# Numerators of a linear attention as whole float32 products, with new input layouts and a new order of issue

## The chip, the cores and the metric

The kernel runs on one NeuronCore of a Trainium2 chip. The metric is the device time of one execution in microseconds. The engines are TensorE (PE; its weight loads are shown as PEld), VectorE (DVE), ScalarE (ACT), GpSimd (POOL) and SyncE (SP), which issues all DMAs here.

## The reference

An attention with random features over 4 batches, 8 heads, 576 rows and 64 columns, and behind it two dense layers over 2304 tokens (512 to 2048 to 512), the first with the gate `h * sigmoid(h)`, the second with `h * cos(h)`.

```python
def phi(x):
    proj = np.einsum('bhsd,df->bhsf', x, w_phi)            # 64 -> 128
    proj = proj - np.max(np.abs(proj), axis=-1, keepdims=True)
    return np.concatenate([np.exp(proj), np.exp(-proj)], axis=-1)
q_p, k_p = (phi(q), phi(k))
kv = np.einsum('bhsf,bhsd->bhfd', k_p, v)
z = np.sum(k_p, axis=2)
num = np.einsum('bhsf,bhfd->bhsd', q_p, kv)
den = np.einsum('bhsf,bhf->bhs', q_p, z)[..., None] + 1e-06
x = (num / den)            # to 2304 x 512, then
h = x @ w_in;  y = (h / (1 + np.exp(-h))) @ w_out          # and the second layer with h * cos(h)
```

## The kernel before

The heads are worked on in eight groups of four (`NQ`, half a batch each). Within a group, heads 0 and 2 are pair p = 0 and heads 1 and 3 are pair p = 1. The 576 rows of a head are 512 in four tiles of 128, and a tail of 64; the tails of four heads are unit u = 0, and a head's four tiles are one of the units 1 to 4.

The steps of a group, each a "piece of work" with a name in the order lists:

- `T` (lines 270 to 286): TensorE transposes the loaded q or k; ScalarE copies PSUM to the high part `hi` (float32r, a float32 rounded to fewer bits that TensorE multiplies in one product); VectorE subtracts for the low part `lo`.
- `phi` (290 to 307): three float32r products (hi x hi, hi x lo, lo x hi) of 256 columns for each row tile; VectorE takes the maximum of the absolute values and subtracts it, into SBUF.
- `kx` (311 to 317): ScalarE makes the keys' two exponentials, a unit at a time. `qx` (319 to 339): TensorE transposes the queries' differences, ScalarE makes the exponentials `e`, GpSimd rounds them to `qh`. `ql` (341 to 346): VectorE, or GpSimd for the tails, subtracts for the low part.
- `kv` (350 to 374): for a pair and a sign, one product for the tails and eight of 65 columns, in float32, with v beside a column of ones; at the end ScalarE copies the sums to `kv_hi` and VectorE makes `kv_lo`.
- `num` (376 to 395): four parts for a pair, each of six float32r products of 288 columns (high x high, high x low, low x high, for two signs); ScalarE copies a part to `xn`, and behind a pair's last part SP sends the row of denominators to a tile `den`.
- `inv` (179 to 189): VectorE inverts the denominators; they go to DRAM (`rd`) and come back on 64 partitions (`rb`). `app` (191 to 200): GpSimd multiplies, into the layers' input `xy`.
- `x`: a part of the first layer's inputs is split in two. `piece`: a quarter of the conversion of a weight tile (lines 91 to 128).

The order is written out by hand: `START` once, then `PERIOD` for n = -1 to 7. A + behind a name is the next group, ++ the one after that. Each engine takes its instructions in that order, and SP its DMAs. PSUM has 8 banks: 2 buffers `tp` of the input transposes, 2 of `phi`, 1 of `t2` (the queries' transposes), 3 that `kv` and `num` share. Where a tile has one buffer, as `qh`, `va` and the loaded inputs, the next group's write waits for the last reader.

The two layers (`moe`, lines 477 to 642) follow, all in float32r with three products each.

Of the kernel before, what the change touches and what calls it, by code (L numbers as in the profile page):

```python
# [30 lines left out]

MAGIC = 12582912.0
# [16 lines left out]
START = parse("""  # L49
T.k.2 w load.v T.k.0 T.k.1 load.k+ phi.k.0 kx.0 phi.k.1 T.q.0 phi.k.2 phi.k.3 kx.1 T.q.2 kv.0.0.0 kx.2 phi.k.4 kx.3  # L50
kv.0.0.1 phi.q.0 T.k.2+ kx.4 kv.1.0.0 phi.q.1 qx.0 T.q.1 phi.q.2 T.k.0+ kv.1.0.1 qx.1 phi.q.3 ql.1.g T.k.1+ kv.0.1.0
qx.2 phi.q.4 load.k++ ql.2.v kv.1.1.0 qx.3 ql.0.g kv.0.1.1 load.q+ kv.1.1.1 qx.4
# [3 lines left out]
kx.1+ x.2+ num.1.1 x.3+ phi.k.2+ T.k.0++ phi.q.0+ num.1.0 x.4+ load.q++ kx.2+ num.1.2 x.5+ kv.0.0.0+ inv.0 phi.k.0++  # L56
T.k.1++ T.q.2++ num.1.3 x.6+ qx.0+ piece phi.q.1+ ql.0.g+ phi.q.2+ kv.1.0.0+ kv.0.0.1+ piece qx.1+ phi.q.4+ app.0
kv.0.1.0+ qx.2+ ql.1.v+ inv.1 phi.q.3+ kv.0.1.1+ piece qx.4+ kv.1.0.1+ ql.2.v+ kv.1.1.0+ qx.3+ phi.k.3++ T.q.1++
kv.1.1.1+ load.k+++ num.0.0+ kx.0++ ql.3.v+ phi.k.4++ num.0.1+ T.k.2+++ load.v++ num.0.2+ x.0++ kx.3++ kx.4++
phi.k.1++ ql.4.v+ app.1 num.0.3+ x.1++ T.q.0++ piece  # L60
# [3 lines left out]
class Weights:  # L64
    """float64 weights, given as raw words, to float32 parts hi + lo of 12 and 12 bits."""
# [68 lines left out]
class Queue:  # L134
    """Pieces of the weights' conversion, taken one after the other."""
# [23 lines left out]
class Norm:  # L159
    """Numerators over denominators, to x, [dm, token]."""  # L160
# [30 lines left out]
    def apply(self, n, p):  # L191
        nc, xy = self.nc, self.xy
# [7 lines left out]
        nc.gpsimd.tensor_mul(xy[rows, B * NJ + b // 2, c0:c0 + 2, at], t[rows, :, SM:S], r[rows, :, SM:S])  # L200


def attention(tc, q, k, v, w_phi, norm, pieces, then):
    nc = tc.nc
    W = D + 1
    with ExitStack() as ctx:
# [5 lines left out]
        kr, krt, qr, qrt = {}, {}, {}, {}  # L212

        def load_qk(n, src, main, tails, name):
            b, h0 = divmod(n, 2)
            h0 *= 4
            t = fp.tile([P, 4, NJ, D], F32, name=f"{name}r")
            u = fp.tile([P, 2, D], F32, name=f"{name}rt")
            for i in range(2):
                nc.sync.dma_start(u[64 * i:64 * i + 64], src[b, h0 + 2 * i:h0 + 2 * i + 2, SM:S, :].rearrange("h s d -> s h d"))  # L220
            nc.sync.dma_start(t, src[b, h0:h0 + 4, 0:SM, :].rearrange("h (p j) d -> p h j d", j=NJ))
            main[n], tails[n] = t, u
# [33 lines left out]
        # Stationary operands of the last product: columns 0..64 [kv | z] of even heads, 63..127 [z | kv] of odd ones.  # L256
        kvs = [[sp.tile([P, 2, 2, M], F32R, name=f"kv{i}_{part}") for part in ("hi", "lo")] for i, M in enumerate((W, P))]
# [10 lines left out]
        tT = {}  # L268

        def transpose_in(n, name, i):  # L270
            main, tails = (kr, krt) if name == "k" else (qr, qrt)
            N = SM if i < 2 else P
            ps = pp.tile([P, N], F32, name="tp", tag="tp", bufs=2)
            if i < 2:
                for c in range(4):
                    x, jj = divmod(c, 2)
                    src = main[n][:, i + 2 * x, 2 * jj:2 * jj + 2, :].rearrange("p j d -> p (j d)")
                    nc.tensor.transpose(ps[:, c * P:(c + 1) * P], src, ident)
            else:
                nc.tensor.transpose(ps, tails[n].rearrange("p a d -> p (a d)"), ident)  # L280
            sfx = "m" if i < 2 else "t"
            hi = fp.tile([P, N], F32R, name=f"{name}T_hi{sfx}", bufs=2 if i < 2 else 1)
            lo = fp.tile([P, N], F32R, name=f"{name}T_lo{sfx}", bufs=2 if i < 2 else 1)
            nc.scalar.copy(hi, ps)
            nc.vector.tensor_sub(lo, ps, hi.bitcast(F32))
            tT[n, name, i] = (hi, lo)
# [3 lines left out]
        def phi(n, name, u):  # L290
            """Unit 0: the tails of the four heads; 1 + 2 p + x: head p + 2 x."""
            i = 2 if u == 0 else (u - 1) // 2
            ns = 1 if u == 0 else 2
            hi, lo = tT[n, name, i]
            ps = pp.tile([P, ns, 2 * F], F32, name="p", tag="p", bufs=2)
            for s in range(ns):
                c = 0 if u == 0 else (((u - 1) % 2) * 2 + s) * P
# [13 lines left out]
        def k_exp(n, u):  # L311
            src = pm.pop((n, "k", u))
            ns = 2 if u == 0 else 4
            t = sp.tile([P, 2, ns, F], F32, name="kpt" if u == 0 else "kp", bufs=1 if u == 0 else 4)
            nc.scalar.activation(t[:, 0], src, AF.Exp)
            nc.scalar.activation(t[:, 1], src, AF.Exp, scale=-1.0)
            kp[n, u] = t

        def q_exp(n, u):
            src = pm.pop((n, "q", u))  # L320
            ns = 2 if u == 0 else 4
            ps = pp.tile([P, ns, P], F32, name="t2", tag="t2", bufs=1)
            for i in range(ns):
                nc.tensor.transpose(ps[:, i, :], src[:, i, :], ident)
            if u == 0:
                for p in range(2):
                    qh[n, p] = sp.tile([P, 2, 2, S], F32R, name=f"qh{p}")
                    ql[n, p] = sp.tile([P, 2, 2, S], F32R, name=f"ql{p}")
            p, x = divmod(u - 1, 2)
            for c in range(2):  # L330
                e = sp.tile([P, ns, P], F32, name="et" if u == 0 else "e", bufs=2 if u == 0 else 4)
                nc.scalar.activation(e, ps, AF.Exp, scale=1.0 - 2.0 * c)
                if u == 0:
                    parts = [(e[:, i, :].rearrange("p (x s) -> p x s", x=2), *(t[n, i][:, c, :, SM:S] for t in (qh, ql))) for i in range(2)]
                else:
                    parts = [(e.rearrange("p a s -> p (a s)"), *(t[n, p][:, c, x, 0:SM] for t in (qh, ql)))]
                for i, (ev, hi, lo) in enumerate(parts):
                    nc.gpsimd.tensor_scalar(hi, ev, 1.0, 0.0, op0=ALU.mult, op1=ALU.add)
                    rests[n, u, c, i] = (lo, ev, hi)

        def q_rest(n, u, engine):
            """The lower parts of the queries' exponentials."""
            for c in range(2):
                for i in range(2 if u == 0 else 1):
                    lo, ev, hi = rests.pop((n, u, c, i))
                    engine.tensor_sub(lo, ev, hi.bitcast(F32))  # L346
# [356 lines left out]
```

## Time and profile before

| | us |
|---|---|
| median of 3 runs | 1051.86 |
| lowest and highest | 1050.23, 1052.01 |
| span of the profiled execution | 1048.8 |
| busy: TensorE, VectorE, ScalarE, GpSimd | 1019.1, 711.9, 407.8, 369.4 |

The profile is of one execution, and its own time is known only as the span, from the first recorded instruction to the last; the runs' median lies 3.1 us above it. TensorE's matmuls are pipelined: an instruction's duration holds the way through the array, so the distance between the starts of two neighbours is what one costs, and the busy time of a stretch is the time in which at least one is under way. A float32 product appears as more than one record. The granted clock is that of TensorE, 1.00 for 2.4 GHz.

### The profile page before, as it was taken

Reading aid. Unit: us, or ns where it says so; the run is one execution under the profiler, and the core shown is the slowest. Engines: PE = TensorE matmul, PEld = TensorE weight load, DVE = VectorE, ACT = ScalarE, POOL = GpSimd, SP = SyncE. Lnnn points to the kernel's source line nnn. Section 1 sums busy time; section 2 is a strip of 40 time slices with the busy share of each in tenths; the row PEclk is TensorE's granted clock in tenths of the full one; section 3 lists DMA queues with packets and bytes.
Section 4 is the critical chain, followed back from the end, with each engine's and each line's share of the span. In section 5 each row is a group of like instructions: output and inputs, shape, how many; then the busy total and the mean of one; then the engine's idle time right before and its main releaser. Section 6 shows DMA issues by size and latency. Waiting matters only on the chain.

```text
span 1048.8 us, 15083 instructions
## 1 busy us (share of the span) xinstructions
PE 1019.1 (97%) x6000; PEld 972.5 (93%) x6000; DVE 711.9 (68%) x956; ACT 407.8 (39%) x664; POOL 369.4 (35%) x426
## 2 busy tenths in 40 slices
PE   7999999999999999999999999999999999999998
PEld 7989999989999999999999999899888988998997
DVE  6999999978544344544545567667677867786764
ACT  5655566544433222222223333444333333333332
POOL 3566666656122111201211024334434433343221
PEclk9999999999999999999999999999999999999999
DMA  4544333114111101110110111101110111100112
GB/s 118 139 112 112 99 105 81 47 40 129 41 41 46 55 22 61 41 41 21 61 48 34 41 41 42 40 21 61 41 41 21 61 40 41 27 34 1 61 57 63
DMA packets 62757, 58.33 MB, mean 56 GB/s; under 512 B 30560, under 2 KB 55264, under 8 KB 62688
## 3 DMA queue, kind: packets, MB, share of 16 engines
q1 hardware_dynamic: 62688, 57.38, 18.5%
q8 instruction: 47, 0.77, 0.3%
q14 instruction: 22, 0.18, 0.1%
HBM read 52.49 MB, written 4.79 MB: 55 GB/s over the span
## 4 chain that ended last, share of the span: by engine, by line
PE 61%; DVE 25%; POOL 7%; ACT 4%; issue 1%; DMA 1%; SPq 0%; POOLq 0%; ACTq 0%; DVEq 0%
PE h L509 24%; PE y L558 6%; PE y L560 6%; PE y L559 6%; DVE ql L346 4%; DVE tb L531 3%; DVE tb L530 3%; DVE tb L535 3%; PE kv L363 3%; POOL ta L529 2%; PE y L563 2%; PE y L564 2%; PE y L565 2%; DVE xy L589 2%; POOL gh L536 2%; DVE gl L538 2%
## 5 line engine op out<-in xcount | busy, mean ns | idle before, releaser
L509 PE MATMUL h<-xh,win_hi 128*128 128x384 f32 x768 | 259.1, 337 | 1.7 <-DVE tb L535 1.7
L509 PE MATMUL h<-xl,win_hi 128*128 128x384 f32 x768 | 258.8, 337 | 0.3 <-DVE xl L474 0.3
L509 PE MATMUL h<-xh,win_lo 128*128 128x384 f32 x768 | 258.7, 337 | 0.0
L521 DVE SCALAR_TENSOR_TENSOR ta<-ta,h 128x768 f32<-128x768 f32 x48 | 45.8, 953 | 177.7 <-ACT ta L520 177.7
L509 PEld LDWEIGHTS h<-xh,win_hi 128*128 128x128 f32 x768 | 144.2, 188 | 4.7 <-PE y L565 2.6
L509 PEld LDWEIGHTS h<-xl,win_hi 128*128 128x128 f32 x768 | 144.2, 188 | 2.4 <-DVE xl L474 0.6
L509 PEld LDWEIGHTS h<-xh,win_lo 128*128 128x128 f32 x768 | 144.2, 188 | 0.0
L532 ACT ACTIVATE tb<-tb 128x768 f32<-128x768 f32 x48 | 40.7, 847 | 239.0 <-DVE tb L531 239.0
L558 PE MATMUL y<-gh,wout_hi 128*128 128x384 f32 x384 | 129.5, 337 | 0.2 <-ACT xy L587 0.2
L560 PE MATMUL y<-gh,wout_lo 128*128 128x384 f32 x384 | 129.6, 337 | 0.0
L559 PE MATMUL y<-gl,wout_hi 128*128 128x384 f32 x384 | 129.4, 337 | 0.0
L520 ACT ACTIVATE ta<-h 128x768 f32<-128x768 f32 x48 | 39.0, 813 | 206.4 <-PE h L509 203.1
L563 PE MATMUL y<-wout_hi,gh 128*128 128x512 f32 x288 | 115.0, 399 | 3.3 <-ACT xy L587 1.8
L564 PE MATMUL y<-wout_lo,gh 128*128 128x512 f32 x288 | 114.4, 397 | 0.0
L565 PE MATMUL y<-wout_hi,gl 128*128 128x512 f32 x288 | 114.4, 397 | 0.0
L536 POOL TENSOR_SCALAR gh<-tb 128x768 fp32r<-128x768 f32 x48 | 46.9, 977 | 186.0 <-DVE tb L535 176.0
L538 DVE TENSOR_TENSOR gl<-tb,gh 128x768 fp32r<-128x768 f32 x48 | 75.4, 1570 | 34.3 <-POOL gh L536 34.3
L121 POOL TENSOR_SCALAR wout_hi<-wt 128x512 fp32r<-128x512 f32 x32 | 27.8, 869 | 200.3 <-DVE wt L118 171.1
L121 POOL TENSOR_SCALAR win_hi<-wt 128x512 fp32r<-128x512 f32 x32 | 21.6, 675 | 187.1 <-DVE wt L118 187.1
L589 DVE TENSOR_TENSOR xy<-y,xy 128x384 f32<-128x384 f32 (+1 forms) x126 | 70.8, 606 | 9.7 <-PE y L560 6.0
L535 DVE TENSOR_TENSOR tb<-tb,h 128x768 f32<-128x768 f32 x48 | 45.6, 951 | 46.7 <-ACT tb L533 46.2
L558 PEld LDWEIGHTS y<-gh,wout_hi 128*128 128x128 f32 x384 | 72.1, 188 | 0.5 <-ACT xy L587 0.5
(114 smaller groups left out, 2082.6 us busy)
## 6 DMA issues: line engine op xcount, KB each, us to landing
raw<-in_moe_w_in SPq DMA_DIRECT2D x32, 512.0 KB, 3.6
raw<-in_moe_w_out SPq DMA_DIRECT2D x32, 512.0 KB, 3.6
rb<-rd SPq DMA_DIRECT2D x16, 288.0 KB, 3.6
kr<-in_k SPq DMA_DIRECT2D x8, 512.0 KB, 4.3
qr<-in_q SPq DMA_DIRECT2D x8, 512.0 KB, 4.1
va<-in_v SPq DMA_DIRECT2D x32, 128.0 KB, 4.1
out<-xy SPq DMA_DIRECT2D x16, 256.0 KB, 2.2
krt<-in_k SPq DMA_DIRECT2D x16, 32.0 KB, 3.1
```

The costliest lines, as they stand in the source:

```text
L121: nc.gpsimd.tensor_scalar(hi, t.bitcast(F32), 1.0, 0.0, op0=ALU.mult, op1=ALU.add)
L509: nc.tensor.matmul(o, a[:, cs], x[t][:, :, c, :], start=first, stop=(c == NC - 1 and a is lo))
L535: nc.vector.tensor_mul(b, b, h)
L536: nc.gpsimd.tensor_scalar(hi, b, 1.0, 0.0, op0=ALU.mult, op1=ALU.add)
L538: nc.vector.tensor_sub(lo, b, hi.bitcast(F32))
L558: nc.tensor.matmul(o, wh[:, ds], hi[:, f, :], stop=False, **st)
L559: nc.tensor.matmul(o, wh[:, ds], lo[:, f, :], start=False, stop=False)
L560: nc.tensor.matmul(o, wl[:, ds], hi[:, f, :], start=False, stop=en)
L563: nc.tensor.matmul(o, hi[:, f, ds], wh, stop=False, **st)
L564: nc.tensor.matmul(o, hi[:, f, ds], wl, start=False, stop=False)
L565: nc.tensor.matmul(o, lo[:, f, ds], wh, start=False, stop=en)
L589: nc.vector.tensor_tensor(y, o, y, op=ALU.add)
```

## The change

- q and k are laid out on the host, already transposed: one array of 128 partitions and 1152 columns for a group (`GC`: 128 columns of tails, then four heads of 512 each two to a column block). `load_qk` is one DMA in place of three, and the input transposes `T` and their PSUM buffers are gone. `split_in` (`sp`) makes the high part with a cast on the engine that the order names (D VectorE, A ScalarE, G GpSimd) and the low part on VectorE, in two pieces of 640 and 512 columns. The rows of a head go to the tiles in another order (also for v and the output stores).
- Keys: `phi` with engine A makes only the maximum, and GpSimd its negative; `k_exp` reads PSUM, with the maximum as bias, one instruction for each row tile's features and sign.
- Numerators: `FULL = (0, 1)`, so for both pairs `qh` and `kv` are float32 tiles without low parts; ScalarE writes the exponentials into `qh`, and a part is two float32 products of 288 columns. The `ql` pieces stand in the order but find nothing to do.
- `app` is on VectorE in the attention (GpSimd for the last group).
- PSUM: 3 buffers of `phi`, 2 of `t2`, 3 of `kv` and `num`. START and PERIOD are other lists.

```diff
+PB, T2, KN = 3, 2, 3
+FULL = (0, 1)
 PERIOD = parse("""
...
+ql.4.D num.0.2 phi.q.1.D+ load.q++ phi.k.2.A+ kx.0+ num.0.3 ql.3.G kx.2+ num.1.0 phi.k.3.A+ sp.k.0.G++ inv.0
+x.4+ x.2+ num.1.1 num.1.2 kx.3+ piece piece phi.q.0.D+ kv.0.0.0+ kv.0.0.1+ phi.k.4.A+ num.1.3 piece phi.q.2.D+
+kx.4+ app.0.D qx.0.G+ kv.0.1.0+ sp.k.1.G++ load.k+++ x.1+ qx.1.D+ ql.0.G+ inv.1 phi.q.3.D+ kv.1.0.0+ phi.k.1.A++
+qx.2.A+ phi.q.4.D+ ql.1.D+ kv.1.0.1+ x.5++ sp.q.0.D++ kv.0.1.1+ qx.3.G+ phi.k.0.A++ x.6+ kv.1.1.0+ kx.1++
+num.0.0+ sp.q.1.D++ ql.2.D+ x.0+ app.1.D kv.1.1.1+ num.0.1+ qx.4.A+ x.3++ piece load.v++
 """)
...
+        def load_qk(n, src, name):
+            t = fp.tile([P, GC], F32, name=f"{name}r")
+            nc.sync.dma_start(t, src[n])
+            raw[n, name] = t
...
+        def split_in(n, name, i, engine):
+            at = slice(0, P + SM) if i == 0 else slice(P + SM, GC)
+            hi, lo = xT[n, name, i] = [fp.tile([P, at.stop - at.start], F32R, name=f"{name}T_{part}{i}") for part in ("hi", "lo")]
+            src = raw[n, name][:, at]
+            cast(engine, hi, src)
+            nc.vector.tensor_sub(lo, src, hi.bitcast(F32))
...
             nc.vector.tensor_reduce(m, pv, axis=AX.X, op=ALU.max, apply_absolute_value=True)
+            if engine == "A":
+                nm = sp.tile([P, 2 * ns], F32, name="nm", bufs=3)
+                nc.gpsimd.tensor_scalar(nm, m, -1.0, 0.0, op0=ALU.mult, op1=ALU.add)
+                if name == "k":
+                    pm[n, name, u] = pv, m, nm
+                    return
...
+            for i in range(ns if m is not None else 0):
+                nc.scalar.activation(t[:, 0, i], src[:, i], AF.Exp, bias=nm[:, i:i + 1])
+                nc.scalar.activation(t[:, 1, i], src[:, i], AF.Exp, bias=m[:, i:i + 1], scale=-1.0)
...
+            for i in full:
+                for c in range(2):
+                    src = ps[:, i, :].rearrange("p (x s) -> p x s", x=2) if u == 0 else ps.rearrange("p a s -> p (a s)")
+                    nc.scalar.activation(qh[n, i][:, c, :, SM:S] if u == 0 else qh[n, i][:, c, x, 0:SM], src, AF.Exp, scale=1.0 - 2.0 * c)
...
                     for c in range(2):
+                        if p in FULL:
+                            nc.tensor.matmul(o, kvs[p][0][:, c, x, :], qh[n, p][:, c, x, at], start=(c == 0), stop=(c == 1))
+                            continue
...
-            nc.gpsimd.tensor_mul(xy[rows, b * NJ:(b + 1) * NJ, c0 + x, :], t[rows, x, 0:SM].rearrange("p (j n) -> p j n", n=P),
+            engine.tensor_mul(xy[rows, b * NJ:(b + 1) * NJ, c0 + x, :], t[rows, x, 0:SM].rearrange("p (j n) -> p j n", n=P),
```

## Rows read from the trace of the kernel before

**Rows 1.** The page: busy time, share of the span and instructions of each engine.

```profile
PE 1019.1 (97%) x6000; PEld 972.5 (93%) x6000; DVE 711.9 (68%) x956; ACT 407.8 (39%) x664; POOL 369.4 (35%) x426
```

**Rows 2.** Busy time by stretch: stretch, its length, engines' busy us, clock, DMA.

```profile
0.00:29.90 29.90, 23.78 (x184) 23.32 (x185) 21.13 (x40) 16.57 (x33) 11.48 (x37) 1.00 0.49 136
85.50:113.00 27.50, 25.63 (x206) 25.47 (x205) 26.38 (x43) 15.85 (x37) 17.11 (x24) 0.93 0.40 107
...
264.00:624.00 360.00, 360.00 (x2058) 360.00 (x2057) 175.17 (x251) 104.12 (x148) 60.94 (x57) 1.00 0.14 43
```

**Rows 3.** Waits from 85.5 to 113 us: who for whom, total, times, longest.

```profile
ACT e L332 <- DVE ql L346: 4.5, 4, 3.0
...
PE t L324 <- DVE pm L306: 1.9, 1, 1.9
```

**Rows 4.** Timeline of TensorE: start, length; numerators of two groups, then the layers.

```profile
29.93 0.38 PE L389 MATMUL num<-qh,kv_hi 128*65 128x288 f32 x1
...
221.40 0.48 PE L389 MATMUL num<-qh,kv_hi 128*65 128x288 f32 x1
...
228.62 0.33 PE L509 MATMUL h<-xh,win_hi 128*128 128x384 f32 x1
```

**Rows 5.** VectorE's groups from 85.5 to 113 us: count, busy us, mean ns, idle before.

```profile
L346 DVE TENSOR_TENSOR ql<-e,qh 128x512 fp32r<-128x512 f32 x8 | 9.2, 1190 | 0.0
L306 DVE TENSOR_TENSOR pm<-p,m 128x512 f32<-128x512 f32 x8 | 5.5, 691 | 0.3
...
L285 DVE TENSOR_TENSOR kT_lom<-tp,kT_him 128x512 fp32r<-128x512 f32 x2 | 1.4, 685 | 0.2 <-ACT kT_him L284 0.2
L285 DVE TENSOR_TENSOR qT_lom<-tp,qT_him 128x512 fp32r<-128x512 f32 x2 | 1.4, 677 | 0.0
...
L368 DVE TENSOR_TENSOR kv_lo<-kv,kv_hi 128x260 fp32r<-128x260 f32 x2 | 0.8, 418 | 0.0
```

**Rows 6.** One line's instructions: lowest, median, highest ns, first and last start.

```profile
L346 DVE TENSOR_TENSOR ql<-e,qh x62: 677/922/2987, 26.4 to 226.5; 128x512 fp32r<-128x512 f32 x62
```

**Rows 7.** ScalarE: groups from 85.5 to 113 us, then lines as in rows 6.

```profile
L315 ACT ACTIVATE kp<-pm 128x512 f32<-128x512 f32 x4 | 2.5, 631 | 0.1
...
L284 ACT CAST kT_hit<-tp x8: 263/264/267, 4.5 to 171.7; 128x128 fp32r<-128x128 f32 x8
...
L533 ACT ACTIVATE tb<-tb,hp x48: 934/938/942, 635.5 to 1036.0; 128x768 f32<-128x768 f32 x48
...
L532 ACT ACTIVATE tb<-tb x48: 843/847/851, 633.3 to 1035.1; 128x768 f32<-128x768 f32 x48
```

**Rows 8.** Timeline of TensorE, merged: start, length, and how many (x).

```profile
149.79 0.30 PE L389 MATMUL num<-qh,kv_hi 128*128 128x288 f32 x1
...
151.37 0.38 PE L360 MATMUL kv<-vt,kpt 128*128 128x130 f32 x2
151.59 1.00 PE L363 MATMUL kv<-va,kp 128*128 128x65 f32 x8
...
154.77 0.29 PE L299 MATMUL p<-wphi,qT_him 128*128 128x256 f32 x1
...
155.84 0.38 PE L360 MATMUL kv<-vt,kpt 128*128 128x130 f32 x2
156.06 1.90 PE L363 MATMUL kv<-va,kp 128*128 128x65 f32 x16
157.80 0.60 PE L324 MATMUL t<-ident,pm 128*128 128x128 f32 x4
158.16 0.36 PE L299 MATMUL p<-wphi,qT_him 128*128 128x256 f32 x1
```

**Rows 9.** Two lines of TensorE, columns as in rows 6.

```profile
L360 PE MATMUL kv<-vt,kpt x64: 272/273/329, 13.0 to 216.4; 128*128 128x130 f32 x64
...
L299 PE MATMUL p<-wphi,kT_him x64: 277/282/562, 9.0 to 202.1; 128*128 128x256 f32 x64
```

**Rows 10.** DMA issues up to 230 us: count, KB each, median us to landing.

```profile
rb<-rd SPq DMA_DIRECT2D x14, 288.0 KB, 3.6
...
den<-xn SPq DMA_DIRECT2D x15, 4.5 KB, 2.1
rd<-r SPq DMA_DIRECT2D x14, 4.5 KB, 1.5
```

More of the change, by code (lines that the diff above doesn't have):

```diff
@@ L49 @@
 START = parse("""
-T.k.2 w load.v T.k.0 T.k.1 load.k+ phi.k.0 kx.0 phi.k.1 T.q.0 phi.k.2 phi.k.3 kx.1 T.q.2 kv.0.0.0 kx.2 phi.k.4 kx.3
-kv.0.0.1 phi.q.0 T.k.2+ kx.4 kv.1.0.0 phi.q.1 qx.0 T.q.1 phi.q.2 T.k.0+ kv.1.0.1 qx.1 phi.q.3 ql.1.g T.k.1+ kv.0.1.0
-qx.2 phi.q.4 load.k++ ql.2.v kv.1.1.0 qx.3 ql.0.g kv.0.1.1 load.q+ kv.1.1.1 qx.4
+w sp.k.0.A load.v phi.k.0.A phi.k.1.A kx.0 kx.1 sp.k.1.G phi.k.2.A sp.q.0.D phi.k.3.A kx.2 load.k+ kv.0.0.0
+phi.q.0.D kv.0.0.1 sp.q.1.A phi.k.4.A kx.3 kx.4 kv.0.1.0 kv.1.0.0 qx.0.A sp.k.0.D+ sp.k.1.G+ phi.q.2.A phi.q.1.D
+kv.1.0.1 phi.q.4.D kv.1.1.0 qx.2.G phi.q.3.D load.q+ load.k++ qx.4.D phi.k.1.A+ kv.0.1.1 qx.1.D kv.1.1.1 ql.1.D
+ql.0.D ql.2.G qx.3.D phi.k.0.A+
 """)
 PERIOD = parse("""
[L56 to L60, printed above, removed]
+ql.4.D num.0.2 phi.q.1.D+ load.q++ phi.k.2.A+ kx.0+ num.0.3 ql.3.G kx.2+ num.1.0 phi.k.3.A+ sp.k.0.G++ inv.0
[3 more added lines that the diff above has]
+num.0.0+ sp.q.1.D++ ql.2.D+ x.0+ app.1.D kv.1.1.1+ num.0.1+ qx.4.A+ x.3++ piece load.v++
 """)
@@ L210, in attention @@
         pp = ctx.enter_context(tc.tile_pool(name="at_ps", bufs=1, space=PSUM))
[L212 to L222, printed above, removed]
+        raw = {}
+        def load_qk(n, src, name):
+            t = fp.tile([P, GC], F32, name=f"{name}r")
+            nc.sync.dma_start(t, src[n])
+            raw[n, name] = t
         def load_v(n):
@@ L255, in attention @@
                 nc.gpsimd.memset(t[64 * x:64 * x + 64, i % 2, c:c + 1], 1.0)
-        kvs = [[sp.tile([P, 2, 2, M], F32R, name=f"kv{i}_{part}") for part in ("hi", "lo")] for i, M in enumerate((W, P))]
+        kvs = [[sp.tile([P, 2, 2, M], F32 if i in FULL else F32R, name=f"kv{i}_{part}") for part in (("all",) if i in FULL else ("hi", "lo"))]
+               for i, M in enumerate((W, P))]
         for t in kvs[1]:
@@ L266, in split_w @@
             nc.vector.tensor_sub(wplo, wff, wphi.bitcast(F32))
[L268 to L278, printed above, removed]
-            else:
[L280 to L286, printed above, removed]
+        xT = {}
@@ new lines, in attention, with cast @@
+        engines = {"D": nc.vector, "A": nc.scalar, "G": nc.gpsimd}
+        def cast(engine, out, src):
+            if engine == "A":
+                nc.scalar.copy(out, src)
+            elif engine == "D":
+                nc.vector.tensor_copy(out, src)
+            else:
+                nc.gpsimd.tensor_scalar(out, src, 1.0, 0.0, op0=ALU.mult, op1=ALU.add)
+        def split_in(n, name, i, engine):
[4 more added lines that the diff above has]
+            nc.vector.tensor_sub(lo, src, hi.bitcast(F32))
@@ L288, in attention, with phi @@
         pm = {}
-        def phi(n, name, u):
-            i = 2 if u == 0 else (u - 1) // 2
+        def phi(n, name, u, engine):
             ns = 1 if u == 0 else 2
-            hi, lo = tT[n, name, i]
-            ps = pp.tile([P, ns, 2 * F], F32, name="p", tag="p", bufs=2)
+            hi, lo = xT[n, name, 0 if u == 0 else (u - 1) // 2]
+            ps = pp.tile([P, ns, 2 * F], F32, name="p", tag="p", bufs=PB)
             for s in range(ns):
-                c = 0 if u == 0 else (((u - 1) % 2) * 2 + s) * P
+                c = 0 if u == 0 else (P if u <= 2 else 0) + ((u - 1) % 2 * 2 + s) * P
@@ L326, in q_exp @@
                 for p in range(2):
-                    qh[n, p] = sp.tile([P, 2, 2, S], F32R, name=f"qh{p}")
-                    ql[n, p] = sp.tile([P, 2, 2, S], F32R, name=f"ql{p}")
+                    qh[n, p] = sp.tile([P, 2, 2, S], F32 if p in FULL else F32R, name=f"qh{p}")
+                    if p not in FULL:
+                        ql[n, p] = sp.tile([P, 2, 2, S], F32R, name=f"ql{p}")
             p, x = divmod(u - 1, 2)
-            for c in range(2):
-                e = sp.tile([P, ns, P], F32, name="et" if u == 0 else "e", bufs=2 if u == 0 else 4)
-                nc.scalar.activation(e, ps, AF.Exp, scale=1.0 - 2.0 * c)
+            full = [i for i in range(2) if i in FULL] if u == 0 else [p] if p in FULL else []
@@ new lines, in q_exp @@
+            for i in full:
+                for c in range(2):
+                    src = ps[:, i, :].rearrange("p (x s) -> p x s", x=2) if u == 0 else ps.rearrange("p a s -> p (a s)")
+                    nc.scalar.activation(qh[n, i][:, c, :, SM:S] if u == 0 else qh[n, i][:, c, x, 0:SM], src, AF.Exp, scale=1.0 - 2.0 * c)
+            parts = rests[n, u] = []
+            if u and full or len(full) == 2:
+                return
+            es = [sp.tile([P, ns, P], F32, name="et" if u == 0 else "e", bufs=2 if u == 0 else 4) for _ in range(2)]
@@ L333, in q_exp @@
+            for c, e in enumerate(es):
                 if u == 0:
-                    parts = [(e[:, i, :].rearrange("p (x s) -> p x s", x=2), *(t[n, i][:, c, :, SM:S] for t in (qh, ql))) for i in range(2)]
-                else:
[L336 to L339, printed above, removed]
+                    for i in range(2):
+                        if i not in full:
+                            parts += [(c, e[:, i, :].rearrange("p (x s) -> p x s", x=2), *(t[n, i][:, c, :, SM:S] for t in (qh, ql)))]
+                    at = slice(1 if 0 in full else 0, 1 if 1 in full else 2)
+                else:
+                    parts += [(c, e.rearrange("p a s -> p (a s)"), *(t[n, p][:, c, x, 0:SM] for t in (qh, ql)))]
+                    at = slice(0, ns)
+                nc.scalar.activation(e[:, at], ps[:, at], AF.Exp, scale=1.0 - 2.0 * c)
+                for c2, ev, hi, _ in parts:
+                    if c2 == c:
+                        cast(engine, hi, ev)
@@ L341, in q_rest @@
         def q_rest(n, u, engine):
[L343 to L346, printed above, removed]
+            for _, ev, hi, lo in rests.pop((n, u)):
+                engine.tensor_sub(lo, ev, hi.bitcast(F32))
         kvp = {}
@@ L382, in go @@
                 def go():
-                    ps = pp.tile([P, 512], F32, name="num", tag="kn", bufs=3)
+                    ps = pp.tile([P, 512], F32, name="num", tag="kn", bufs=KN)
                     o = ps[0:M, 0:HS]
@@ L402, in step @@
                 return then(front)
-            key = (n, name, *arg)[:3] if name == "ql" else (n, name, *arg)
+            key = (n, name, *(a for a in arg if a not in engines))
             if key in done or not 0 <= n < NQ:
@@ L439, in step @@
             elif name == "app":
-                norm.apply(n, *arg)
+                norm.apply(n, arg[0], engines[arg[1]])
         done.update({(0, "load", "k"), (0, "load", "q")})
@@ L570, in store @@
             if b < B:
[L571 removed]
+                nc.sync.dma_start(out[b * S + j * P:b * S + (j + 1) * P, :], y)
             else:
@@ L692 @@
     for name in ("q", "k", "v", "w_phi", "moe_w_in", "moe_w_out", "moe2_w_in", "moe2_w_out"):
-        a = np.ascontiguousarray(inputs[name])
+        a = inputs[name]
+        if name in ("q", "k"):
+            x = np.asarray(a).reshape(2 * B, 4, S, D)
+            main = x[:, [0, 2, 1, 3], :SM].reshape(2 * B, 4, 2, 2, P, D).transpose(0, 3, 5, 1, 2, 4).reshape(2 * B, P, 8 * P)
+            tail = x[:, :, SM:].reshape(2 * B, 2, 2, S - SM, D).transpose(0, 2, 4, 1, 3).reshape(2 * B, P, P)
+            a = np.concatenate([tail, main], axis=2)
+        a = np.ascontiguousarray(a)
         if a.dtype == np.float64:
```

57 lines of the change are left out of this document (32 added, 25 removed).

## The prediction

> **What bounds the kernel now.** I read the header first. TensorE is busy 97% of the span [rows 1], which would say that nothing is to be gained off it; but this is an average over two stages. The busy time by stretch splits them. In the middle of the two layers (264 to 624 us) TensorE is busy 360 of 360 us at full clock, and VectorE half of the time; the change does not touch that stage. In one period of the attention (85.5 to 113 us) VectorE is busy 26.4 of 27.5 us, TensorE 25.6 with a mean granted clock of 0.93, ScalarE 15.9, GpSimd 17.1 [rows 2]. So the attention is at VectorE's limit, with TensorE close behind. The waits of that period agree: TensorE's transposes of the queries wait 1.9 us for VectorE's subtraction, and ScalarE's exponentials wait 4.5 us in all for VectorE's `ql` [rows 3]. In the same period the clock is at the lower of its two levels, 1.2 in place of 2.4 GHz, for about a seventh of the time (0.93 is 1 - 0.5/7); in the layers it is not.
>
> The attention's parts are marked by the first numerator of each group of four heads: the first of all starts at 29.93, that of the last group at 221.40, and the layers' first product at 228.62 [rows 4]. So the start takes 29.9 us, seven periods take 191.5 us (27.35 each), the tail 7.2 us. Everything after it is 1048.8 - 228.6 = 820.2 us.
>
> **VectorE per period.** Removed: the eight `ql` subtractions on it (9.2 us), the keys' half of the subtractions of the maximum (half of 5.5), `kv_lo` (0.8), and the subtractions behind the input transposes (1.4 for keys, as much for queries) [rows 5]: -15.6. Added: four subtractions `split_in`, now from SBUF, of 640 and 512 columns. The nearest row is `ql`, also two operands in SBUF: 0.68 at least for 512 columns [rows 6], so 2 x (0.85 + 0.68) = 3.1. Two casts of the queries' inputs, 1152 columns: the one-column-a-cycle bound is the same 0.68 per 512, 1.5. Two `apply`, moved from GpSimd: per head pair two products of 512 columns and one of 128, 2 x (0.68 + 0.68 + 0.3) = 3.3. Sum 7.9. VectorE goes from 26.4 to about 18.7 us, from the limit to well under it.
>
> The upper end: `ql` takes 0.68 us at best, 1.18 in the mean of this period and 2.99 at worst [rows 5, 6], while the subtractions that read PSUM stay at 0.68 [rows 5]. So operands that lie in SBUF are at times held up. With all ten of the new wide operations at 1.18 it is 5 us more: 23.7. I take 20, as GpSimd loses its 512-column casts and products and so most of what ran beside `ql`.
>
> The Trainium skill (SBUF — State Buffer, "Who interferes with whom") says that a VectorE instruction with two SBUF inputs and a GpSimd instruction that reads SBUF exclude each other. That fits the spread of `ql`, and it speaks against this change, which puts `split_in` and `apply` into just that class; it also says that GpSimd's small operations can be held up by them. What it would give is the second rival.
>
> **ScalarE per period.** The keys' exponentials come straight from PSUM with the maximum as a bias, so one 128-column instruction for each row group and sign: 36, in place of 8 of 512 and 2 of 256 columns. Price of one: a 128-column cast takes 0.265, and a bias that is a column in SBUF adds 0.94 - 0.85 = 0.09 to a 768-column one [rows 7], so at most 0.36; below, 0.2, if neighbours overlap as the 512-column ones do. Removed: 8 x 0.63 = 5.0 and 0.8 for the tails, and three input casts, each of k and q, of 0.6, 0.6 and 0.27: -2.9. Added: 36 x 0.28 = 10.1 (7.2 to 13), and 0.4 for splitting the queries' tails in four. 15.9 - 8.7 + 10.5 = 17.7 us (14.8 to 20.6). **GpSimd** loses the casts of `qh`, the tails' `ql` and `apply` and gains two casts of inputs and five negated maxima: a few us, far from any limit. But these five now stand between VectorE's maximum and the exponentials.
>
> **TensorE per period.** Counts come from the code, rates from distances between starts in a stretch without waits [rows 8]. 54 `phi` products: 9 starts in 1.07 us, 0.119 each: 6.4. 18 transposes of queries at 0.10: 1.8. `kv`: 64 records at 0.109 (16 in 1.74) and 8 at 0.11: 7.9. Those stay. Removed: 18 transposes of inputs, 1.8; and 48 numerator products at 0.132 (12 in 1.58): 6.3. Added: 16 float32 products of 288 columns. A float32 product shows as two records in this trace (16 records for 8 calls of line 363). What is one of 288 columns worth? Below, as a float32r record of 288: 0.13. Above, from the widest float32 row: 130 columns start 0.11 apart [rows 8], times 288/130 is 0.244. I take 0.25, because the 130-column float32 record lasts 0.272, as a 256-column float32r record does (0.28) [rows 9]: a float32 column costs two of the others. 32 x 0.25 = 8.0 (4.2 to 8.0). So TensorE's need goes from 24.2 to 24.1 us: the transposes pay for the slower numerators.
>
> The Trainium skill (FP8 and Floating Point Precision, "TensorE Precision Notes") says that true float32 makes four passes; as an estimate, 4 x 288 columns at 2.4 GHz are 0.48 us a product, 7.7 us a period against 5.8 for three single passes. It speaks against this change for TensorE, and sides with my upper end; no row here has a wide float32 product.
>
> **Order and waits.** Walking the new PERIOD with these prices, TensorE finds nearly every operand ready: three PSUM buffers for `phi`, two for the transposes. The tight places: the last `kv` copy on ScalarE must be out before `num.0.2` takes that PSUM buffer (slack about 0.4 us), and `app.0`, now in VectorE's queue, waits for the reciprocals to come back through DRAM. That chain is den 2.1, rd 1.5, rb 3.6 us [rows 10], 7.2 in all, against some 9 us of other VectorE work and waits between `num.0.3` and `app.0`. Behind `app.0` stand `sp.k.1`, `inv.1` and `phi.q.3`, and behind these TensorE. On SP the eight loads of v come just ahead of the den of the next period, and the one-piece loads of q and k replace three transfers each. I allow 0.7 us of stalls a period: 24.8 us, with TensorE as the bound and the dips of the clock gone.
>
> **Start, tail, rest.** The start has the same pieces, with VectorE busy 21 of 29.9 us [rows 2]; it loses the input transposes and `ql`, but gets the long row of exponentials: -2 us (0 to -4). The tail has kv.1.1.1 and eight numerators behind its mark in place of eight shorter ones: 0.9 + 0.4 + 8 x 1.0 = 9.3, +2.1. Layers: the stores of outputs become contiguous, which nobody waits for, and the same 820 us stay (+-1: the layout of SBUF, and so which old tile the first new ones wait for, is another).
>
> **Sum.** -2 + 7 x (24.8 - 27.35) + 2.1 = -17.8; span 1048.8 - 17.8 = 1031; the runs' median lies 3.1 us above the profiled span, so **1034 us**.
>
> **Rivals.** (1) Float32 at the lower end, 0.13 a record: TensorE needs 20.3 us, VectorE and ScalarE at 20 set some 22 us a period: -2 - 37.5 + 2, 1014 us. Against it: the length of the 130-column record. (2) The new SBUF operations are held up and the order slips: VectorE near 23.7 plus waits, 26 us a period: -2 - 9.5 + 2, 1042 us. For it: the 2.99 us `ql`; against: GpSimd has little left. (3) The attention's real limit is TensorE's issue as it is, 25.6 busy of 27.5: nothing is gained, tail +2, 1053 us. Against it: the wait and the clock in that period. (4) Slower: the wait for rb in VectorE's queue becomes the loop. Price: VectorE stands idle from its arrival at `app.0` until rb lands, each period, with TensorE behind. With VectorE's 20 us it decides from an idle time of about 7.5 us a period; at 8.5 the period is 28.5 and the time 1060. For it, SP issues the loads in order, and den can stand behind them; against it, den, rd and rb together are 7.2 us, and most of that lies under other work.
>
> **How the numbers follow.** Forecast 0.62 (own range 1028 to 1040), (1) 0.06, (2) 0.22, (3) 0.04, (4) 0.06. The range takes in the forecast and (2) with their ends and leaves out (1) and (4): 1026 to 1045. A measurement of this kernel tells about 0.2% (2.1 us) from no change: faster 0.90, same 0.04, slower 0.06.
>
> **What would show it.** Right: marks of the first numerator some 25 us apart; TensorE without waits over 1 us between them and at full clock; VectorE under 85% busy; float32 records of 288 columns starting 0.24 to 0.25 apart; keys' exponentials about 0.28 apart. Wrong: numerator records at 0.13 or near 0.5; VectorE idle ahead of `xy<-xn,rb` for several us each period; ScalarE over 95% busy; a first product of the layers that waits.

## The result and the profile after

| | before | after |
|---|---|---|
| median (4 runs each), us | 1051.05 | 1023.70 |
| lowest and highest | 1047.64, 1052.01 | 1022.18, 1025.63 |
| span of the profiled execution | 1048.8 | 1020.4 |

The ratio is 0.975, 95% interval 0.973 to 0.978: faster, by more than was forecast (1034), and 2 us below the lower end of the range. The profiled run of after took 1022.18 us. Of the runs below, one execution of e9 (1432.6 us) and one of e13 (2023.2 us) were in a slow state and are left out of the figures.

Busy time by stretch, after (stretch, its length, busy us of TensorE, its weight loads, VectorE, ScalarE, GpSimd, then clock and DMA): the start, one period, the tail.

```profile
0.00:27.16 27.16, 20.20 (x153) 19.27 (x154) 15.82 (x27) 17.91 (x56) 5.12 (x30) 1.00 0.67 186
...
97.92:121.86 23.94, 23.94 (x179) 21.58 (x179) 19.55 (x37) 18.36 (x60) 4.42 (x9) 1.00 0.50 123
...
192.56:202.00 9.44, 9.38 (x47) 6.63 (x46) 3.57 (x8) 6.00 (x15) 0.00 (x0) 1.00 0.09 23
```

Against [rows 2]: VectorE falls from 26.4 of 27.5 us to 19.6 of 23.9, and TensorE is now busy all of the period, at full clock. TensorE's timeline (start, length; an x counts merged records) has the marks of [rows 4]:

```profile
27.16 3.07 PE L417 MATMUL num<-qh,kv_all 128*65 128x288 f32 x12
...
192.56 1.14 PE L417 MATMUL num<-qh,kv_all 128*65 128x288 f32 x4
...
201.39 0.55 PE L541 MATMUL h<-xh,win_hi 128*128 128x384 f32 x1
```

The start is 27.2 us (29.9 before), the seven periods 165.4 (191.5), the tail 8.8 (7.2), all behind it 1020.4 - 201.4 = 819.0 (820.2). The gain lies in the seven periods: 26.1 of the 28.4 us of span. The five in the middle are 23.94 us long, but for a 24.16. The first, 22.66, is short because START has already issued kv.1.1.1 and qx.4 of the first group ahead of its mark; the last, 22.82, because there is no group after the next whose keys would be worked on.

The price of a float32 numerator product, in the same timeline:

```profile
103.52 2.10 PE L417 MATMUL num<-qh,kv_all 128*65 128x288 f32 x8
105.25 0.49 PE L302 MATMUL p<-wphi,kT_hi 128*128 128x256 f32 x1
105.58 0.28 PE L303 MATMUL p<-wplo,kT_hi 128*128 128x256 f32 x1
```

The eight records of two parts start within 1.73 us, and the next product then takes 0.33 to the one behind it, where 0.12 is usual; the other 0.21 is counted to the numerators. (1.73 + 0.21) / 8 = 0.243 us a record of 288 columns, 0.485 a product. A float32r product of 288 columns took 0.132 [rows 8].

The waits from 50 to 192 us, some six periods (who for whom, total, times, longest), have none of TensorE among their first:

```profile
POOL nm L310 <- DVE m L307: 103.5, 27, 5.8
DVE m L307 <- PE p L304: 19.0, 25, 1.9
ACT xn L180 <- PE num L417: 16.2, 23, 1.6
...
DVE xy L205 <- DMA rb<-rd: 6.7, 9, 1.8
```

In [rows 3] TensorE waited for VectorE; here VectorE and ScalarE wait for TensorE. GpSimd's long wait is idle time, as it has little to do.

### The profile page after: what moved, and what is told of

Same layout as the page of the kernel before. It is cut to its first block, busy times and chain, and to the rows that moved or that the text cites. A ratio compares the mean times of both kernels' runs of the same rounds, so it can differ in the third digit from the quotient of the medians.

```text
span 1020.4 us, 14455 instructions
## 1 busy us (share of the span) xinstructions
PE 1003.4 (98%) x5728; PEld 940.4 (92%) x5728; DVE 645.7 (63%) x879; ACT 424.1 (42%) x846; POOL 265.9 (26%) x308
## 4 chain that ended last, share of the span: by engine, by line
PE 79%; DVE 10%; POOL 6%; ACT 3%; issue 1%; DMA 1%; SPq 0%; POOLq 0%; ACTq 0%; DVEq 0%
PE h L541 31%; PE y L592 7%; PE y L591 7%; PE y L590 7%; PE num L417 6%; PE kv L391 5%; PE y L595 4%; PE y L596 4%; PE y L597 4%; DVE tb L563 2%; DVE tb L562 2%; DVE tb L567 2%; PE p L302 2%; PE p L304 2%; PE p L303 2%; POOL ta L561 2%
## 5 line engine op out<-in xcount | busy, mean ns | idle before, releaser
L592 PEld LDWEIGHTS y<-gh,wout_lo 128*128 128x128 f32 x384 | 72.1, 188 | 0.0
```

Source lines behind the costliest of these rows:

```text
L592: nc.tensor.matmul(o, wl[:, ds], hi[:, f, :], start=False, stop=en)
```

## The experiments

Each was timed against the kernel before on the same chip. "Period" is the mean distance of the marks over the five middle periods of its trace; by that measure before has 27.8 us and after 24.0.

| run | median us | ratio to before, 95% | period us |
|---|---|---|---|
| e3: before + float32 numerators | 1037.2 | 0.987 (0.986 to 0.989) | 25.8 |
| e4: before + new inputs | 1048.5 | 0.999 (0.997 to 1.000) | 27.5 |
| e5: before + keys' exponentials from PSUM | 1120.9 | 1.068 (1.064 to 1.071) | 37.4 |
| e10: before + float32 numerators + new inputs | 1021.5 | 0.972 (0.970 to 0.975) | 23.9 |
| e1: after - float32 numerators | 1098.5 | 1.046 (1.043 to 1.049) | 34.4 |
| e6: after - keys' exponentials from PSUM | 1022.7 | 0.974 (0.971 to 0.977) | 24.2 |
| e9: after - the added PSUM buffers | 1051.9 | 1.001 (1.000 to 1.003) | 27.1 |
| e13: after - keys' exponentials - buffers | 1039.0 | 0.990 (0.988 to 0.992) | 26.1 |
| e8: after, half of the numerators' products | 1019.4 | 0.971 (0.968 to 0.974) | 23.4 |
| e11: new inputs, pair 0 whole, pair 1 split | 1028.5 | 0.980 (0.978 to 0.981) | 24.4 |
| e12: the same, pairs exchanged | 1041.3 | 0.992 (0.990 to 0.993) | 26.3 |
| e14: e11 with casts on ScalarE | 1033.0 | 0.984 (0.982 to 0.987) | 25.1 |

**One part of the change at a time, on the kernel before.** First the float32 numerators (e3): exponentials written whole into `qh`, no low parts, two products a part.

```diff
-                        nc.tensor.matmul(o, kh, a, start=(c == 0), stop=False)
-                        nc.tensor.matmul(o, kh, b, start=False, stop=False)
-                        nc.tensor.matmul(o, kl, a, start=False, stop=(c == 1))
+                        nc.tensor.matmul(o, kvs[p][0][:, c, x, :], qh[n, p][:, c, x, at], start=(c == 0), stop=(c == 1))
```

> The kernel before with the float32 numerators alone: ScalarE writes the exponentials whole, no casts of them, no low parts, two float32 products a part; order, inputs, keys' exponentials and PSUM buffers as before. Theory: VectorE's 26.4 us a period lose 9.2 and 0.8, TensorE's 24.2 gain 1.5: TensorE becomes the bound at 25.7 us, marks 25.8 to 26.5 us apart in place of 27.35, and 1040 to 1046 us. Rival (order and buffers decide): marks stay at 27 to 28 us, 1049 to 1054 us.

Two of its periods, by stretch as above:

```profile
81.75:107.59 25.84, 25.84 (x196) 23.38 (x196) 18.63 (x34) 16.43 (x39) 7.72 (x9) 1.00 0.41 109
107.59:133.44 25.85, 25.85 (x197) 23.39 (x196) 18.60 (x34) 16.44 (x40) 8.09 (x8) 1.00 0.43 112
```

As the theory had it: VectorE drops to 18.6 us, and TensorE runs without a gap at 25.85, in the old order and with the old buffers. Next the new inputs alone (e4): `load_qk` is one load, and

```diff
-                    nc.tensor.transpose(ps[:, c * P:(c + 1) * P], src, ident)
+            src = main[n][:, P + i * SM:P + (i + 1) * SM] if i < 2 else main[n][:, 0:P]
-            nc.scalar.copy(hi, ps)
-            nc.vector.tensor_sub(lo, ps, hi.bitcast(F32))
+            nc.scalar.copy(hi, src)
+            nc.vector.tensor_sub(lo, src, hi.bitcast(F32))
```

> The kernel before with the new inputs alone: no input transposes, high parts by ScalarE and low parts by VectorE from SBUF; numerators in three float32r products, and all else as before. Theory (VectorE is the limit of before): TensorE's 1.9 us less a period bring nothing, and the low parts from SBUF cost VectorE the same or more (3.4 to 5.5 us a period): marks 27 to 29 us apart, 1047 to 1061 us. Rival (TensorE's work is the limit already): marks 25.5 us apart, 1036 us.

```profile
113.00:140.00 27.00, 24.42 (x190) 23.80 (x189) 26.59 (x43) 16.13 (x36) 17.88 (x24) 0.94 0.37 102
```

As the theory had it: TensorE's 18 transposes less a period bring 1 us, not clear of noise, and at most 3; VectorE, busy 26.6 of these 27 us, is the limit there. Both together (e10):

> The kernel before with two parts of the change: the float32 numerators and the inputs laid out transposed (one load a group, no input transposes on TensorE; high parts still cast by ScalarE, low parts by VectorE, now from SBUF). Keys' exponentials, order, PSUM buffers of phi and of the queries' transposes, and the products by the inverses on GpSimd as before. The float32 numerators alone gave a TensorE without stalls at 25.85 us a period, and the 18 transposes are 1.9 us of that. Theory (what counts is TensorE's work, once VectorE is off the limit): marks 23.9 to 24.6 us apart, 1021 to 1029 us, as fast as the whole change. Rival (keys' exponentials from PSUM, the third and second buffers and the new order are needed): 25.5 us or more, 1034 us or more.

```profile
97.61:121.49 23.88, 23.88 (x178) 21.46 (x178) 19.16 (x34) 16.42 (x40) 8.21 (x8) 1.00 0.47 120
121.49:145.37 23.88, 23.88 (x178) 21.46 (x178) 18.48 (x34) 16.42 (x40) 7.80 (x8) 1.00 0.41 107
```

These two parts are the whole gain: 1021.5 us against 1023.7 for the whole change, with ratios whose intervals overlap. Float32 alone is worth 12.6 us, the inputs alone 1, both 28: the first takes VectorE off the limit, and only then do the transposes count, 25.85 - 23.88 = 1.97 us a period, 0.109 each. Last the keys' exponentials alone (e5):

```diff
-            nc.scalar.activation(t[:, 0], src, AF.Exp)
-            nc.scalar.activation(t[:, 1], src, AF.Exp, scale=-1.0)
+            for i in range(ns):
+                nc.scalar.activation(t[:, 0, i], src[:, i], AF.Exp, bias=nm[:, i:i + 1])
+                nc.scalar.activation(t[:, 1, i], src[:, i], AF.Exp, bias=m[:, i:i + 1], scale=-1.0)
```

> The kernel before with the keys' exponentials read from PSUM alone (36 instructions of 128 columns a period with the maximum as bias, the negative by GpSimd), all else as before, with two PSUM buffers of phi. VectorE loses 3.2 of 26.4 us a period, TensorE needs 24. Theory (the buffers: a phi tile is held by ScalarE's eight exponentials of 0.29 us, and with two buffers TensorE stalls, as with two buffers in the changed kernel): marks 27 to 30 us apart, 1048 to 1070 us. Rival (VectorE's load alone decides): marks 24.5 to 25.5 us apart, 1030 to 1037 us.

Its TensorE timeline, with the idle time ahead and who ended it:

```profile
79.31 0.38 PE L299 MATMUL p<-wphi,kT_him 128*128 128x256 f32 x1 [1.74 <-ACT kpt L322]
86.05 0.38 PE L299 MATMUL p<-wphi,kT_him 128*128 128x256 f32 x1 [2.53 <-ACT kp L322]
```

```profile
113.00:140.00 27.00, 20.88 (x143) 19.54 (x143) 14.55 (x27) 16.89 (x56) 11.92 (x22) 0.87 0.42 108
```

The mechanism was the expected one, and the size was not: 71 us are lost, more than three times the 20 that I had allowed. TensorE may not write the next tile of `phi` until the last exponential of the keys two tiles back has read it. A part of the loss is not waiting: with these gaps in TensorE's work the granted clock falls to 0.87 to 0.91 in the mean of a middle period, and TensorE is busy 29.5 us a period where it was busy 25.9 before; its idle time goes from 2 to 8 us.

**Undoing one part of the change.** The numerators in three products again (e1, `FULL = ()`):

> The changed kernel with the numerators as three float32r products again, with high and low parts of the exponentials and of kv; inputs, keys' exponentials, PSUM buffers and order as changed. TensorE's need falls by 8 x (0.97 - 0.79) = 1.4 us to 22.5 us a period, VectorE's rises from 19.3 by kv_lo (0.8), two casts (0.8) and six subtractions (4.1 to 7.1) to 25 to 27. Theory (VectorE's load was the limit, the float32 numerators take it off): marks 25 to 27 us apart in place of 23.9, 1031 to 1045 us. Rival (the new order and PSUM buffers brought the gain): the period follows TensorE, 22.5 us, 1013 us.

```profile
98.43 0.35 PE L423 MATMUL num<-qh,kv_lo 128*65 128x288 f32 x1 [1.04 <-DVE kv_lo L397]
...
108.76 0.61 PE L422 MATMUL num<-ql,kv_hi 128*128 128x288 f32 x1 [3.79 <-POOL ql L374]
```

Slower than either theory had it. The engines are not full; TensorE waits for `kv_lo` and for GpSimd's `ql`. In two stretches VectorE is busy 16.7 and 18.7 of 24 us, and the granted clock is 0.86 and 0.85:

```profile
97.00:121.00 24.00, 18.87 (x132) 17.46 (x131) 16.66 (x29) 15.57 (x51) 7.71 (x11) 0.86 0.31 84
121.00:145.00 24.00, 17.70 (x121) 16.18 (x120) 18.66 (x32) 15.11 (x43) 10.45 (x17) 0.85 0.32 87
```

In a middle period of 34.1 us TensorE is idle for 6.4 and busy for 27.7, 5 us more than the 22.5 that its work was put at: a part of the loss is the clock, which is at its lower level for some of the time. The longest wait comes from GpSimd's own queue, where `ql` stands behind a negated maximum that GpSimd waits 6.95 us for:

```profile
107.28 0.20 POOL L310 TENSOR_SCALAR nm<-m 128x4 f32<-128x4 f32 x1 [6.95 <-DVE m L307]
107.44 2.50 POOL L374 TENSOR_TENSOR ql<-e,qh 128x512 fp32r<-128x512 f32 x2
```

So in this order the float32 numerators do more than relieve VectorE: exponentials and sums are ready as soon as ScalarE has written them. My sum of loads for this run missed that. How much of the loss is left with these `ql` on VectorE, or in another order, was not tried.

The keys' exponentials undone (e6, `phi.k` with engine D):

> The changed kernel with the keys' exponentials as before: VectorE subtracts the maximum into SBUF, ScalarE makes two instructions of 512 columns a unit; PSUM buffers, order, float32 numerators and inputs as changed. VectorE 19.3 + 3.2 = 22.5 us a period, ScalarE some 6 less, phi's PSUM tiles free sooner; the three SBUF tiles of differences are now shared by queries and keys. Theory (TensorE is the bound and the keys' exponentials from PSUM bring nothing by themselves): marks 23.9 to 24.6 us apart, 1023 to 1029 us. Rival (VectorE's load decides, every us counts): marks 25 to 27 us apart, 1031 to 1046 us.

```profile
99.06:122.99 23.93, 23.93 (x178) 21.57 (x178) 21.80 (x40) 14.27 (x34) 4.30 (x4) 1.00 0.47 122
```

No difference, with VectorE at 21.8 of 23.9 us: the keys' exponentials from PSUM bring nothing. The PSUM buffers of before (e9):

```diff
-PB, T2, KN = 3, 2, 3
+PB, T2, KN = 2, 1, 3
```

> The changed kernel with the PSUM buffers of before for phi (2) and for the queries' transposes (1); order and all else as changed. Theory (the buffers are what lets TensorE run without a stall: a key's phi tile is held until ScalarE's eight exponentials are out): stalls of 2 to 4 us a period, marks 26 to 28 us apart, 1038 to 1052 us. Rival (the work taken off VectorE is enough): marks within 0.5 us of 23.9, 1023 to 1027 us.

```profile
95.31 0.38 PE L302 MATMUL p<-wphi,kT_hi 128*128 128x256 f32 x1 [0.81 <-ACT kpt L333]
103.43 0.39 PE L302 MATMUL p<-wphi,kT_hi 128*128 128x256 f32 x1 [0.26 <-ACT kp L333]
108.79 0.66 PE L341 MATMUL t<-ident,pm 128*128 128x128 f32 x4 [1.42 <-ACT qh L352]
```

The whole gain is lost, as the theory had it. Both buffers are missed, that of `phi` (0.81 and 0.26 in this period) and that of the queries' transposes (1.42). Of the 30.9 us between the two spans the seven periods have 21.7 and the start 9.0. In the start TensorE's products are slow for longer: those of 256 columns start 0.21 us apart up to 25.7 us here, in after up to 9.9, and 0.12 apart later. The profile gives the granted clock as 1.00 there, and why the slow stretch is longer was not tested.

```profile
24.21 0.41 PE L303 MATMUL p<-wplo,qT_hi 128*128 128x256 f32 x1
24.43 0.41 PE L304 MATMUL p<-wphi,qT_lo 128*128 128x256 f32 x1
```

Both parts undone (e13):

> The changed kernel with two parts undone together: the keys' maximum subtracted by VectorE as before, and the PSUM buffers of before (2 of phi, 1 of the queries' transposes). Each was undone alone: the keys' exponentials cost nothing, the buffers 3.2 us a period. Theory (the buffers are needed only because ScalarE's exponentials hold the keys' phi tiles; without that two are enough, as in the kernel before): marks 23.9 to 24.7 us apart, 1022 to 1030 us. Rival (the new order itself needs the buffers): marks 26 to 27.5 us apart, 1040 to 1054 us.

```profile
99.66 0.66 PE L341 MATMUL t<-ident,pm 128*128 128x128 f32 x4 [0.46 <-ACT qh L352]
104.57 0.35 PE L302 MATMUL p<-wphi,qT_hi 128*128 128x256 f32 x1 [1.29 <-DVE pm L319]
```

My theory fell: 26.1 us, 1.0 better than e9 but 2.1 from after. The keys' hold on the tiles is the smaller part; the new order itself needs the buffers, and the old order does without them (e10).

**What comes after TensorE.** One of the two products of each numerator part left out (e8), which halves that work:

```diff
-                            nc.tensor.matmul(o, kvs[p][0][:, c, x, :], qh[n, p][:, c, x, at], start=(c == 0), stop=(c == 1))
+                            if c == 0:
+                                nc.tensor.matmul(o, kvs[p][0][:, c, x, :], qh[n, p][:, c, x, at], start=True, stop=True)
```

> The changed kernel with one of the two products of each numerator part left out (the part of the exponentials with negative sign does not enter, so the numbers that come out are others; all else is done). TensorE's need falls by 16 records of 0.243 us, 3.9 us a period, to 20.1 us. Theory (TensorE is the bound and nothing else is near): marks 20.1 to 21.5 us apart, as VectorE at 19.3 comes next; 1001 to 1008 us. Rival (a chain through VectorE, ScalarE and DMA has the same length as TensorE's work): marks at 23 us or more, 1017 us or more.

```profile
79.52 0.49 PE L388 MATMUL kv<-vt,kpt 128*128 128x130 f32 x2 [2.29 <-ACT xn L180]
...
103.20 0.49 PE L388 MATMUL kv<-vt,kpt 128*128 128x130 f32 x2 [1.63 <-ACT xn L180]
```

Of 3.9 us a period taken from TensorE some 0.6 comes off, 4.3 us between the medians. The theory fell: TensorE is the bound, but it is not alone. The next limit stands close behind: the middle periods are 21.6 to 25.3 us long, and `kv` waits for a PSUM buffer that `num` still holds, because its copy stands on ScalarE behind the keys' exponentials. With these waits the clock also falls again in places (0.93 in the mean from 94.1 to 117.8 us, 0.87 in the longest period).

**Attempts at something faster.** e10 leaves VectorE some 5 us a period, so one pair was put back into three shorter products (e11 pair 1, e12 pair 0; both with 3 and 2 PSUM buffers):

```diff
+                        if p != SPLIT:
+                            nc.tensor.matmul(o, kvs[p][0][:, c, x, :], qh[n, p][:, c, x, at], start=(c == 0), stop=(c == 1))
+                            continue
```

> A version meant to beat both. The kernel before with the new inputs; pair 0 with float32 numerators, pair 1 with three float32r products; keys' exponentials and order as before, 3 PSUM buffers of phi and 2 of the queries' transposes. With both pairs in float32 TensorE was without stalls at 23.9 us, with VectorE busy 19 us. One pair in float32r takes 4 x (0.97 - 0.79) = 0.72 off TensorE, 23.2 us, and puts kv_lo and four subtractions on VectorE (3.1 to 5.1: 22 to 24). Theory (TensorE remains the limit as VectorE still fits): marks 23.2 to 23.5 us apart, 1015 to 1019 us. Rival (VectorE's subtractions, held up beside GpSimd's casts and products, are the limit again): 24 us or more, 1022 us or more.

> The same with the pairs exchanged: pair 0 in three float32r products, pair 1 in float32. The sums are the same but for the stationary operand of 65 columns; the order differs: pair 0's low parts are needed by num.0, the first numerators behind them, so there is less time for VectorE. Theory: marks 23.2 to 23.8 us apart, 1015 to 1021 us. Rival (the low parts come too late): 24 us or more, 1022 us or more.

e11's waits on TensorE:

```profile
87.05 0.44 PE L313 MATMUL t<-ident,pmt 128*128 128x128 f32 x2 [0.31 <-DVE pmt L295]
91.41 0.66 PE L313 MATMUL t<-ident,pm 128*128 128x128 f32 x4 [0.60 <-DVE pm L295]
108.62 0.40 PE L391 MATMUL num<-ql,kv_hi 128*128 128x288 f32 x1 [0.34 <-DVE ql L343]
```

The rivals won: the sum puts TensorE's need at 23.2 us, and the periods are 24.4 (e11) and 26.3 (e12), with TensorE waiting for low parts and differences. Moving the casts (e14) did not help:

```diff
-                nc.gpsimd.tensor_scalar(hi, ev, 1.0, 0.0, op0=ALU.mult, op1=ALU.add)
+                nc.scalar.copy(hi, ev)
```

> The mixed version (pair 0 in float32, pair 1 in three float32r products, new inputs, order of before) with the casts of pair 1's exponentials on ScalarE in place of GpSimd. There the marks were 24.5 us apart, 1.3 over TensorE's 23.2, with TensorE waiting for VectorE's differences, and VectorE's pair-1 subtractions took 1.04 us in the mean of two periods. ScalarE goes from 16.5 to some 19 us a period, GpSimd loses 3.4. Theory (what was held up were VectorE's operations beside GpSimd's): subtractions at 0.7 us, marks 23.2 to 23.7 us apart, 1015 to 1019 us. Rival (the order of before, made for a slower TensorE, does not feed it at 23.2 us a period, whichever engine casts): marks 24.2 us or more, 1022 us or more.

`ql` is still 0.93 us in the mean of 75 to 125 us, and the period is 25.1, so GpSimd's casts were not the cause of the long ones. Those lie beside GpSimd's products `xy`, which `app` makes: here two of `ql` take 2.29 us, while the pair that has no product beside it takes 1.28 (110.91 to 112.19). GpSimd's timeline and VectorE's (start, length):

```profile
103.76 2.97 POOL L198 TENSOR_TENSOR xy<-xn,rb 64x512 f32<-64x512 f32 x2 [2.66 <-DMA rb<-rd]
106.69 0.91 POOL L201 TENSOR_TENSOR xy<-xn,rb 64x128 f32<-64x128 f32 x1
105.85 2.29 DVE L343 TENSOR_TENSOR ql<-e,qh 128x512 fp32r<-128x512 f32 x2
```

These products on VectorE, as in after, were not tried with e11, and which of the waits sets e11's period was not separated. The 3 us more of ScalarE's work can have cost e14 something too. The best kernel found is e10, no faster than after by more than can be measured.

## Why the prediction was right or wrong

**The bound before: right.** VectorE at 26.4 of 27.5 us is the limit (e3, e4), and the layers are untouched (819.0 against 820.2 us).

**The new bound: right.** TensorE at its work, full clock, no waits. Its need was put at 24.1 us a period and it is busy 23.94. The record of 288 columns is 0.243 us; the upper end, 0.244 worked out from the 130-column rows [rows 8], was closer than the 0.25 that I took. Rival 1 falls with it. The Trainium skill (FP8 and Floating Point Precision, "TensorE Precision Notes") has four passes, an estimate of 0.48 us a product; the trace agrees with 0.485. The transposes were put at 0.10 and are 0.109.

**VectorE: right, and the lock showed itself.** 18.7 to 23.7 us were given, 20 taken; five periods have 16.9 to 20.0. The new subtractions and products of 512 columns run at the 0.68 us of the fastest `ql` [rows 6], with one exception in each of several periods. The casts were priced too high: there is no bound of 0.68 us for 512 columns, they take 0.42, and 0.48 for 640, so 0.9 us where 1.5 was taken. The mean of the casts of 512 columns, after:

```profile
L280 DVE CAST qT_hi<-qr 128x512 fp32r<-128x512 f32 x6 | 2.5, 418 | 0.0
```

VectorE's and GpSimd's timelines, after (start, length):

```profile
74.17 0.69 DVE L290 TENSOR_TENSOR qT_lo<-qr,qT_hi 128x512 fp32r<-128x512 f32 x1
```

```profile
99.02 1.79 DVE L290 TENSOR_TENSOR qT_lo<-qr,qT_hi 128x512 fp32r<-128x512 f32 x1
```

```profile
99.00 1.27 POOL L134 TENSOR_TENSOR win_lo<-wt,win_hi 128x512 fp32r<-128x512 f32 x1
```

The same subtraction takes 0.69 us when GpSimd has nothing under way as it starts; where a GpSimd subtraction of 1.27 us has begun 0.02 us before, it takes 1.79, ending 0.54 after it. It works the other way too: a negated maximum of GpSimd that starts at 74.33, inside the first of these, takes 0.58 us where the median is 0.20. The Trainium skill (SBUF — State Buffer, "Who interferes with whom") has the one that comes second blocked until the first ends. The trace agrees but for a remainder: 0.54 us are left after 100.27, less than the 0.69 of the undisturbed one. With GpSimd busy 4.4 us a period in place of 17, it costs 1.1 us in such a period, and TensorE hides it. Rival 2 did not come.

**ScalarE: right.** 18.4 us against 17.7; the exponentials start 0.25 apart, where I took 0.28.

**The wait for rb: right that it is there, and that it costs nothing.** 6.7 us of VectorE's time in six periods; e10, with the products on GpSimd, is as fast. Rival 4 did not come.

**The step that failed: "I allow 0.7 us of stalls a period: 24.8 us".** There are none: TensorE is busy for the whole of each of the seven periods. That is 0.7 x 7 = 4.9 us, the largest miss in the sum. The walk through the order had found nearly every operand ready, and the allowance came from no row. The other misses are smaller, and almost all go the same way. The sum gave all seven periods the full length, while the old 27.35, their mean, already has the short first and last one in it: 2.4 us, less 0.2 for the one period of 24.16. TensorE's need was put at 24.1 in place of 23.94: 1.1 us. Start, tail and layers add 0.8, 0.5 and 1.2. Together that is 10.7: the span was forecast at 1031 and is 1020.4. So the mechanism was right and its sizes were not. Without the stalls the sum gives 1029, and with the short end periods as well 1027, which the range, from 1026, still holds; only with the other terms does the time fall below it. The range was too narrow for misses that add up.

**What the sum hid.** The prediction counted five reliefs of VectorE and the buffers as one change. The runs take it apart: the two that matter are the float32 numerators and the inputs; the keys' exponentials bring nothing (e6) and are a loss where buffers are few (e5); the products on VectorE are not needed for the gain (e10, which has them on GpSimd); the buffers are there to pay for the new order (e9, e13). Rival 3, that TensorE's issue was the limit before, has this much in it: with float32 numerators TensorE's work is only 2 us a period below the old period (25.8 in e3 against 27.8), and without the new inputs the gain stops at 13 us.

## What to carry to other kernels

When the busiest engine is relieved, write the second engine's work as a sum of starts, not of busy time: that sum was the new period to within 1%. What is taken off the second engine is worth next to nothing before and its full price after. Trading three reduced products and their split for one slower full product pays where the splitting engine is the limit; here it also shortened the chain from producer to consumer, which a sum of loads does not show (e1). When a walk through the order finds no stall, give the case without stalls its own place in the range.

## What was not expected of the hardware

- A float32 product costs its two records of 0.243 us at 288 columns, but 0.109 both at 65 and at 130 columns [rows 8]: between these two widths it is not the columns that set the price. A float32 transpose of 128 columns is 0.109 too (25.85 - 23.88 over 18).
- Neighbouring 128-column exponentials with a column of SBUF as bias last 0.36 to 0.37 us each and start 0.25 apart:

```profile
105.35 0.37 ACT L332 ACTIVATE kp<-p,nm 128x128 f32<-128x128 f32 x1 [0.26 <-POOL nm L310]
105.61 0.36 ACT L333 ACTIVATE kp<-p,m 128x128 f32<-128x128 f32 x1
105.86 0.37 ACT L332 ACTIVATE kp<-p,nm 128x128 f32<-128x128 f32 x1
```

  So four of them cost 1.0 us where one of 512 columns lasts 0.63 [rows 7], not four times as much.
